# Value products with heads and rests side by side in an attention and MoE kernel

## The chip, the cores and the metric

The kernel runs on one core of a Trainium2 chip. The metric is the device time of one execution in microseconds (us). Engines are named as the profile names them: PE is TensorE's matrix product, PEld its weight load, DVE is VectorE, ACT is ScalarE, POOL is GpSimd and SP is SyncE, which here issues nearly all transfers.

## The reference

Eight batches of eight heads, 512 local and 32 global tokens with 64 elements each. Global queries see all 544 keys, local queries see the 32 global keys and the local keys within 32 positions. All outputs, laid out as 4352 tokens of 512 elements, go through a layer of 2048 with a squared ReLU.

```python
out_g = np.matmul(sm(s_g), v_all)
...
mask = np.abs(pos[:, None] - pos[None, :]) <= window
s_ll = np.where(mask, s_ll, -1000000000.0)
s_l = np.concatenate([s_lg, s_ll], axis=-1)
out_l = np.matmul(sm(s_l), np.concatenate([v_g, v_l], axis=2))
out = np.concatenate([out_g, out_l], axis=2)
...
h = np.maximum(x @ w_in, 0.0)
return (h * h @ w_out).astype(np.float32)
```

## The kernel before

The work is cut into 128 "heads" `t`: a batch, a half of its 512 local queries (256 queries) and one of eight heads. One pass of the main loop is an iteration `t`. In it the kernel computes the scores of head `t`, the transposes and value products of head `t - 1`, and one step `m = t - 9` of the second part, which works on blocks of 256 tokens: eight steps to a block, each with 256 of the 2048 hidden elements (`gemm1`, `act1`, `act2`) and the second layer of the step before (`gemm2`).

Precision comes from splitting. A float32 tensor is written as a head, its value rounded to `fp32r` (a cast on ACT, named `hi`, `ph`, `gh`, `x_h`), and a rest, the difference (a subtraction on DVE, named `lo`, `pl`, `gl`, `x_l`). A product is then head times head, head times rest, and rest times head. The first 16 heads (`plain`) are computed in plain float32 without splits.

For one head from 16 on, the steps are:

- `split_head`: ACT casts the packed queries, keys and values (864 columns) to `hi`; DVE subtracts to make `lo` (448 columns: queries and 192 value columns), the rest of the keys in the lower 64 partitions, and the rest of the global values (32 partitions, 64 columns).
- `scores`: four products into the PSUM tile `s`.
- `softmax1` on DVE (mask, maximum), `softmax2` on ACT (two exponentials with sums), `softmax3` on DVE (reciprocal, two multiplications of 224 columns).
- `transposes` on PE into the one PSUM tile `pt`; `pt_split` on ACT copies the heads to `ph` (four copies), `pt_rest` on DVE makes the rests (`pl`, and parts of `ph`).
- `av`: nine products into the PSUM tile `xa`, six of 128 columns for the two halves, two of 128 and one of 256 columns for the middle keys and the globals.
- `x_evac`: ACT copies `xa` to `x_h`, DVE subtracts to `x_l`; these feed `gemm1`.

The global queries of four heads are handled together, with 16 such groups in all. `g_soft`, `g_exp`, `g_norm`, `g_tr`, `g_tr_last`, `g_rest`, `g_split_v`, `g_av` (13 products of 128 columns) and `g_x` are "jobs", spread over the iterations after the group's last scores by a table of iteration and place. `gt` and `gxo`, the global tiles in PSUM, use the same single buffer (tag `xa`) as the local products.

PE, ACT and DVE run independently, each its own queue in order. From iteration 17 on (`FREE`) each keeps the order in which the program is written; before that a scheduler may reorder. Weights of the second part are decoded and split in the first iterations by a written plan (`PLAN`). `SQ` says in which of 16 iterations the square in `act1` is taken by ACT; in the others DVE multiplies. The order within one iteration, by engine, for heads from 17 on:

```python
# PE:  transposes(t-1), scores(t), gemm1(m,0), gemm1(m,1), av(t-1), g_scores(t), gemm2(m-1)
# ACT: pt_split(t-1), softmax2(t), act1(m), x_evac(t-1), split_head(t+1), g_evac(t), act2(m)
# DVE: softmax1(t), pt_rest(t-1), softmax3(t), act1(m), x_evac(t-1), split_head(t+1), g_evac(t), act2(m)
```

Jobs at place 4 follow `pt_split`, those at 3 follow `pt_rest`, those at 2 stand ahead of `gemm2` and `act2`, those at 1 end the iteration. Every eighth iteration `evac` copies a finished block `o` out on ACT, ahead of `softmax3`.

Of the kernel before, what the change touches and what calls it, by code (L numbers as in the profile page):

```python
# [16 lines left out]
P = 128  # L17
# [14 lines left out]
LOOK = 2  # L32
SQ = (2, 3, 4, 5, 14, 15)
MUL = 9
# [3 lines left out]
def f(ap):  # L38
    return ap.bitcast(F32)
# [19 lines left out]
def attention_moe(  # L59
# [65 lines left out]
    def split_head(t):  # L125

        hd = heads[t]
        raw = hd["raw"]
        if plain(t):
            return  # L130
        hi = p2.tile([P, PK], F32R, tag="hi", name=f"hi{t}")
        lo = p2.tile([P, QC + 192], F32R, tag="lo", name=f"lo{t}")
        ac.copy(hi, raw)
        ve.tensor_sub(lo, raw[:, KC : KC + QC + 192], f(hi[:, KC : KC + QC + 192]))
        ve.tensor_sub(hi[64:, :KC], raw[64:, :KC], f(hi[64:, :KC]))
        ve.tensor_sub(hi[32:64, PK - 64 :], raw[32:64, PK - 64 :], f(hi[32:64, PK - 64 :]))
        hd["hi"], hd["lo"] = hi, lo
# [47 lines left out]
    def softmax3(t):  # L185
        st = heads[t]["st"]
        pr = prob[t % 2]
        ve.tensor_scalar(out=st[:, 6:8], in0=st[:, 4:6], scalar1=1e-9, scalar2=None, op0=ALU.add)
        ve.reciprocal(out=st[:, 0:2], in_=st[:, 6:8])
        for u in range(2):  # L190
            w_ = pr[:, WIN * u : WIN * (u + 1)]
            if MUL <= t < NPLAIN:
                ac.activation(out=w_, in_=w_, func=AF.Copy, scale=st[:, u : u + 1])
            else:
                ve.tensor_scalar(out=w_, in0=w_, scalar1=st[:, u : u + 1], scalar2=None, op0=ALU.mult)
# [6 lines left out]
    def pt_split(t):  # L202
        hd = heads[t]
        if plain(t):
            pts = p2.tile([P, 512], F32, tag="gh", name=f"pts{t}")
            ac.copy(pts, pt)
            hd["pts"] = pts
            return
        ph = p1.tile([P, 640], F32R, tag="ph", name=f"ph{t}")
        pl = p1.tile([P, 256], F32R, tag="pl", name=f"pl{t}")  # L210
        ac.copy(ph[:, :256], pt[:, :256])
        ac.copy(ph[:64, 256:384], pt[:64, 320:448])
        for r in (0, 32):
            ac.copy(ph[r : r + 32, 384:640], pt[64:96, 256:512])
        hd["ph"], hd["pl"] = ph, pl

    def pt_rest(t):
        if plain(t):
            return
        ph, pl = heads[t]["ph"], heads[t]["pl"]  # L220
        ve.tensor_sub(pl, pt[:, :256], f(ph[:, :256]))
        ve.tensor_sub(ph[64:, 256:384], pt[:64, 320:448], f(ph[:64, 256:384]))

        ve.tensor_sub(ph[64:, 384:640], pt[64:, 256:512], f(ph[:64, 384:640]))

    def av(t):
        hd = heads[t]
        c = QC + KC
        if plain(t):

            xa = ps_a.tile([P, HALF], F32, tag="xa", name=f"xa{t}")
            v, pts = hd["raw"][:, c:], hd["pts"]
            mm = [
                (xa, v[:, 0:128], pts[:, 256:512]),
                (xa[:, 0:128], v[:, 64:192], pts[:, 0:128]),
                (xa[:, 128:256], v[:, 128:256], pts[:, 128:256]),
            ]
        else:
            xa = ps_a.tile([64, HALF], F32, tag="xa", name=f"xa{t}")
            vh, vl, ph, pl = hd["hi"][:, c:], hd["lo"][:, QC:], hd["ph"], hd["pl"]  # L240
            mm = []
            for u in range(2):
                o, vs, ps = xa[:, 128 * u : 128 * u + 128], slice(64 * u, 64 * u + 64), slice(128 * u, 128 * u + 128)
                mm += [(o, vh[:, vs], ph[:, ps]), (o, vl[:, vs], ph[:, ps]), (o, vh[:, vs], pl[:, ps])]
            o = xa[:, 64:192]
            mm += [(o, vh[:, 128:192], ph[:, 256:384]), (o, vl[:, 128:192], ph[:, 256:384])]
            mm.append((xa, vh[:, 192:256], ph[:, 384:640]))
        for i, (o, a, b) in enumerate(mm):
            pe.matmul(o, a, b, start=i == 0, stop=i == len(mm) - 1, skip_group_check=True)
        hd["xa"] = xa[:64, :]  # L250

    def x_evac(t):
# [3 lines left out]
        if g == 0:  # L256
            ac.copy(xg[r, h // 2, :], xa)
        else:
            ac.copy(x_h[r, g % 2, h // 2, :], xa)
            ve.tensor_sub(x_l[r, g % 2, h // 2, :], xa, f(x_h[r, g % 2, h // 2, :]))  # L260
        heads[t] = None
# [3 lines left out]
    def g_load(t):  # L265
# [7 lines left out]
        if plain(t):  # L273
            qz = p1.tile([P, 512], F32, tag=("ph", "gvl", "gvh", "ph")[t // 4], name=f"qz{t}")
            nc.gpsimd.memset(qz, 0.0)
# [42 lines left out]
    def g_split_v(t, pair):  # L318

        gv = state["gv"]  # L320
        gvh = p1.tile([P, 5, P], F32R, tag="gvh", name=f"gvh{t}_{pair}")
        gvl = p1.tile([P, 4, P], F32R, tag="gvl", name=f"gvl{t}_{pair}")
        ac.copy(gvh, gv)
        ve.tensor_sub(gvl, gv[:, :4, :], f(gvh[:, :4, :]))
        ve.tensor_sub(gvh[32:64, 4, :], gv[32:64, 4, :], f(gvh[32:64, 4, :]))
        state["gvs"] = gvh, gvl

# [11 lines left out]
    def g_norm(t):  # L339
        s, st = sg[:, (t // 4) % 2, :], state["gst", t]  # L340
        for o in (544, 576):
            ve.tensor_copy(out=s[:, o : o + 32], in_=s[:, 512:544])
        ve.tensor_scalar(out=st[:, 3:4], in0=st[:, 2:3], scalar1=1e-9, scalar2=None, op0=ALU.add)
        ve.reciprocal(out=st[:, 0:1], in_=st[:, 3:4])
        ve.tensor_copy(out=st[:64, 1:2], in_=st[64:, 0:1])

    def g_tr(t):
# [3 lines left out]
        for c in range(4):  # L351
            pe.transpose(gt[:, 128 * c : 128 * c + 128], s[:, 128 * c : 128 * c + 128], ident)
        pth = p1.tile([P, 640], F32R, tag="pth", name=f"pth{t}")
        ac.copy(pth[:, :512], gt)
        state["gpt"] = pth, gt

# [8 lines left out]
    def g_rest(t):  # L365
        (pth, gt), ge = state["gpt"], state["ge"]
        ptl = p1.tile([P, 512], F32R, tag="ptl", name=f"ptl{t}")
        ac.copy(pth[:64, 512:], ge[:64, :])
        ve.tensor_sub(ptl, gt, f(pth[:, :512]))
        ve.tensor_sub(pth[64:, 512:], ge[64:, :], f(pth[:64, 512:]))  # L370
        state["gpt"] = pth, ptl

    def g_av(t, pair):
        (gvh, gvl), (pth, ptl) = state["gvs"], state["gpt"]
        xo = ps_a.tile([64, P], F32, tag="xa", name=f"gxo{t}_{pair}")
        mm = []
        for c in range(4):
            cols = slice(128 * c + 64 * pair, 128 * c + 64 * pair + 64)
            mm += [(pth[:, cols], gvh[:, c, :]), (pth[:, cols], gvl[:, c, :]), (ptl[:, cols], gvh[:, c, :])]
        mm.append((pth[:, 512 + 64 * pair : 576 + 64 * pair], gvh[:, 4, :]))  # L380
        for i, (x, y) in enumerate(mm):
            pe.matmul(xo, x, y, start=i == 0, stop=i == len(mm) - 1)
        xs = p1.tile([64, P], F32, tag="xs", name=f"gxs{t}_{pair}")
        ac.activation(out=xs, in_=xo, func=AF.Copy, scale=state["gst", t][:64, pair : pair + 1])
        state["xs"] = xs
# [56 lines left out]

    def gemm1(m, j):
        blk, st = divmod(m, 8)
# [11 lines left out]
        for n, (a, b) in enumerate(mm):  # L456
            pe.matmul(hp[:, j, :], a, b, start=n == 0, stop=n == len(mm) - 1)

    def act1(m):
# [3 lines left out]
        ac.activation(out=r, in_=hp, func=AF.Relu)  # L463
        if m < 8 or m + LAG < NT + 8 and (m + LAG) % 16 in SQ:
            ac.activation(out=r, in_=r, func=AF.Square)
# [37 lines left out]
    def evac(blk, tiles=(0, 1)):  # L503
        for i in tiles:
            pool, tag = ((p1, "ot"), (p2, "gl"))[i]
            ot = pool.tile([P, DM], F32, tag=tag, name=f"ot{blk}_{i}")
# [82 lines left out]
    for t in range(NSTEP + LAG + 1):  # L589
# [32 lines left out]
        if live and early:  # L622
            g_scores(t)
        if run:
            gemm1(m, 1)
        if prev:
            av(t - 1)
        if live and not early:
            g_scores(t)
        if early and t + 1 < NPLAIN:  # L630
            scores(t + 1)
        if live and not early:
            softmax3(t)
# [137 lines left out]
```

## Time and profile before

| | |
|---|---|
| median of 3 runs | 1068.78 us (1068.65 to 1068.86) |
| profiled execution | 1068.82 us, span 1067.0 us |
| granted TensorE clock | 1.000 |
| busy PE / PEld | 1050.4 / 941.7 us |
| busy DVE / ACT / POOL | 856.3 / 753.1 / 3.9 us |
| moved by DMA | 96.78 MB, mean 91 GB/s |

The span is the time from the first to the last instruction of the program. Busy time is the union of an engine's instructions. Since nearly every instruction is issued through one helper, almost all rows carry line 52 (`L52`), and one reads them by the names of the tiles: `ph<-pt` is an instruction that writes `ph` and reads `pt`. Shapes are partitions times elements. In lists of groups, a row gives the busy time of the group, the mean duration of one instruction in ns, and the idle time of the engine ahead of it with what ended it.

### The profile page before, as it was taken

To read this page: it belongs to the slowest core of one execution; us is meant where nothing else is said; L and a number is where in the kernel's file an instruction comes from. 1 tells how busy PE (TensorE), PEld (TensorE's weight loads), DVE (VectorE), ACT (ScalarE), POOL (GpSimd) and SP (SyncE) were. 2 spreads that over 40 slices of the span, in tenths; PEclk is the share of its full clock that TensorE was granted. 3 is DMA by queue.
4 is the path that set the end of the run, shared out by engine and by line. 5 is a ranking of instruction groups with operands and counts; after the bars stand their busy time and mean duration, and the time that the engine had idled before them with its cause. 6 is when DMAs were issued, how large, how long until landed. Compare 5 with 4: busy or idle time off the path is not lost.

```text
span 1067.0 us, 21142 instructions
## 1 busy us (share of the span) xinstructions
PE 1050.4 (98%) x7568; PEld 941.7 (88%) x7568; DVE 856.3 (80%) x2687; ACT 753.1 (71%) x1901; POOL 3.9 (0%) x14
## 2 busy tenths in 40 slices
PE   7999999999999999999999999999999999999998
PEld 6776889999998989998999989999999989999896
DVE  5698988898888989988888888888888888874321
ACT  5898877778777776778777777777777787774322
POOL 1000000000000000000000000000000000000000
PEclk9999999999999999999999999999999999999999
DMA  9772132223222322222322222223221322201000
GB/s 372 310 263 74 57 106 76 71 80 98 68 89 64 103 65 83 74 91 77 94 71 82 86 72 76 90 66 100 78 89 55 94 86 66 88 29 33 13 20 20
DMA packets 54312, 96.78 MB, mean 91 GB/s; under 512 B 4288, under 2 KB 29376, under 8 KB 54208
## 3 DMA queue, kind: packets, MB, share of 16 engines
q1 hardware_dynamic: 54064, 95.37, 27.2%
q8 instruction: 60, 0.98, 0.4%
q14 instruction: 44, 0.36, 0.1%
q10 hardware_dynamic: 144, 0.07, 0.0%
HBM read 86.51 MB, written 8.91 MB: 89 GB/s over the span
## 4 chain that ended last, share of the span: by engine, by line
PE 87%; ACT 7%; DVE 4%; issue 1%; DMA 0%; ACTq 0%
PE o L52 33%; PE h L52 32%; PE xa L52 7%; PE s L52 6%; PE pt L52 5%; PE gxo L52 2%; PE gs L52 2%; ACT prob L52 1%; DVE prob L52 1%; ACT r L52 1%; ACT ph L52 1%; ACT hi L52 1%; ACT ot L52 1%; PE gt L52 1%; ACT sg L52 0%
## 5 line engine op out<-in xcount | busy, mean ns | idle before, releaser
L52 PE MATMUL h<-x_h,ws 128*128 128x256 f32 x2048 | 388.9, 283 | 0.0
L52 PEld LDWEIGHTS h<-x_h,ws 128*128 128x128 f32 x2048 | 327.0, 191 | 0.5
L52 PE MATMUL o<-ws,gh 128*128 128x512 f32 x1024 | 321.3, 395 | 0.0
L52 PE MATMUL h<-x_l,ws 128*128 128x256 f32 x1024 | 289.1, 282 | 0.1
L52 PEld LDWEIGHTS o<-ws,gh 128*128 128x128 f32 x1024 | 185.5, 188 | 34.6
L52 PE MATMUL o<-ws,gl 128*128 128x512 f32 x512 | 202.6, 396 | 0.0
L52 PEld LDWEIGHTS h<-x_l,ws 128*128 128x128 f32 x1024 | 195.9, 191 | 0.9 <-DVE x_l L52 0.4
L52 ACT CAST ph<-pt 128x256 fp32r<-128x256 f32 x448 | 141.1, 341 | 67.7 <-PE pt L52 60.8
L52 ACT ACTIVATE prob<-prob,st 128x224 f32<-128x224 f32 x270 | 127.8, 475 | 61.2 <-DVE st L52 59.1
L52 ACT ACTIVATE r<-h 128x512 f32<-128x512 f32 x136 | 81.4, 599 | 112.3 <-PE h L52 112.3
L52 PEld LDWEIGHTS o<-ws,gl 128*128 128x128 f32 x512 | 96.2, 188 | 22.7
L52 DVE CUSTOM_DVE_ANT_0 prob<-s,con 128x224 f32<-128x224 f32 x256 | 90.0, 386 | 24.5 <-PE s L52 23.2
L52 DVE TENSOR_TENSOR gl<-r,gh 128x512 fp32r<-128x512 f32 x128 | 87.9, 686 | 23.3 <-ACT gh L52 20.5
L52 ACT CAST hi<-raw 128x864 fp32r<-128x864 f32 x112 | 102.5, 915 | 1.4
L52 DVE TENSOR_TENSOR r<-h,r 128x512 f32<-128x512 f32 x82 | 56.7, 692 | 51.9 <-ACT r L52 50.6
L52 PE MATMUL xa<-ph,hi 128*64 128x128 f32 x448 | 87.3, 238 | 1.6 <-DVE ph L52 1.2
L52 DVE TENSOR_TENSOR hi<-raw,hi 64x352 fp32r<-64x352 f32 x224 | 82.5, 368 | 6.4
L52 ACT CAST gh<-r 128x512 fp32r<-128x512 f32 x128 | 79.1, 618 | 9.1 <-DVE r L52 8.7
L52 DVE TENSOR_TENSOR ph<-pt,ph 64x128 fp32r<-64x128 f32 x224 | 79.6, 355 | 7.0
L52 DVE TENSOR_TENSOR lo<-raw,hi 128x448 fp32r<-128x448 f32 x112 | 69.6, 622 | 15.3 <-ACT hi L52 12.5
L52 PE MATMUL pt<-con,prob 128*128 128x128 f32 (+1 forms) x512 | 78.2, 274 | 0.7 <-ACT prob L52 0.5
L52 DVE TENSOR_SCALAR prob<-prob,st 128x224 f32<-128x224 f32 x242 | 70.7, 334 | 4.1
(80 smaller groups left out, 1572.7 us busy)
## 6 DMA issues: line engine op xcount, KB each, us to landing
raw<-in_pk_dram SPq DMA_DIRECT2D x127, 432.0 KB, 3.2
wr<-in_w_dram SPq DMA_DIRECT2D x32, 512.0 KB, 7.9
gv<-in_vg_dram SPq DMA_DIRECT2D x32, 320.0 KB, 3.3
out_dram<-ot SPq DMA_DIRECT2D x32, 256.0 KB, 2.2
qr<-in_qg_dram SPq DMA_DIRECT2D x31, 64.0 KB, 2.8
out_dram<-ot SPq DMA_DIRECT2D x8, 64.0 KB, 1.7
con<-in_consts_dram SPq DMA_DIRECT2D x2, 224.0 KB, 5.1
raw<-in_pk_dram SPq DMA_DIRECT2D x1, 304.0 KB, 3.2
```

The lines of the kernel that those rows point to most:

```text
L52: r = method(*args, **kwargs)
```

## The change

The value products get their head and rest stored side by side. `pt_split` and `pt_rest` write one tile `ps` of 896 columns in which head and rest of 128 columns alternate, `split_head` writes heads and rests of the values in strips of 64, and one product with a 128-wide weight (head and rest of the values) and a 256-wide moving operand (head and rest of the probabilities) replaces three. `av` then has four products into a 128-partition `xa`, and the partial sums stand in three places, which `x_evac` adds on DVE: one subtraction and two additions in place of one subtraction. `g_av` has five products, and two additions (`g_add`) follow.

Moved: `av` stands between two halves of `gemm1(m, 1)`; `split_head(t + 1)` and `x_evac(t - 1)` stand ahead of `act1`; all squares of iterations up to 127 are taken by ACT, those after it by DVE; the second multiplication of `softmax3` goes to ACT for the split heads; the global scaling becomes `g_mul` on ACT, in place of the scale in the copy of `gxo`; the output staging tile shares a buffer with the global `pth`; one early `qz` uses another buffer.

```diff
-        hi = p2.tile([P, PK], F32R, tag="hi", name=f"hi{t}")
-        lo = p2.tile([P, QC + 192], F32R, tag="lo", name=f"lo{t}")
-        ac.copy(hi, raw)
-        ve.tensor_sub(lo, raw[:, KC : KC + QC + 192], f(hi[:, KC : KC + QC + 192]))
+        c = QC + KC
+        hi = p2.tile([P, c + 2 * VC + QC], F32R, tag="hi", name=f"hi{t}")
+        lo = hi[:, c + 2 * VC :]
+        vr = raw[:, c:].rearrange("p (b n) -> p b n", b=4)
+        vs = hi[:, c : c + 2 * VC].rearrange("p (b n) -> p b n", b=4)
+        ac.copy(hi[:, :c], raw[:, :c])
+        ac.copy(vs[:, :, :64], vr)
+        ve.tensor_sub(lo, raw[:, KC:c], f(hi[:, KC:c]))
         ve.tensor_sub(hi[64:, :KC], raw[64:, :KC], f(hi[64:, :KC]))
-        ve.tensor_sub(hi[32:64, PK - 64 :], raw[32:64, PK - 64 :], f(hi[32:64, PK - 64 :]))
+        ve.tensor_sub(vs[:, :, 64:], vr, f(vs[:, :, :64]))
...
-            if MUL <= t < NPLAIN:
+            if MUL <= t < NPLAIN or t >= NPLAIN and u == 1:
                 ac.activation(out=w_, in_=w_, func=AF.Copy, scale=st[:, u : u + 1])
...
-        ac.copy(ph[:, :256], pt[:, :256])
-        ac.copy(ph[:64, 256:384], pt[:64, 320:448])
-        for r in (0, 32):
-            ac.copy(ph[r : r + 32, 384:640], pt[64:96, 256:512])
+        ps = p1.tile([P, 896], F32R, tag="ph", name=f"ph{t}")
+        pb = ps[:, :512].rearrange("p (u h n) -> p u h n", u=2, h=2)
+        ac.copy(pb[:, :, 0, :], pt[:, :256].rearrange("p (u n) -> p u n", u=2))
+        ac.copy(ps[:64, 512:640], pt[:64, 320:448])
+        ac.copy(ps[:64, 640:], pt[64:, 256:])
...
+        ve.tensor_sub(pb[:, :, 1, :], pt[:, :256].rearrange("p (u n) -> p u n", u=2), f(pb[:, :, 0, :]))
+        ve.tensor_sub(ps[64:, 512:640], pt[:64, 320:448], f(ps[:64, 512:640]))
+        ve.tensor_sub(ps[64:, 640:], pt[64:, 256:], f(ps[:64, 640:]))
...
+            xa = ps_a.tile([P, 512], F32, tag="xa", name=f"xa{t}")
+            xb = xa.rearrange("p (u h n) -> p u h n", u=2, h=2)
+            ps, vs = hd["ps"], [hd["hi"][:, c + 128 * i : c + 128 * i + 128] for i in range(4)]
+            both = bass.AP(xa.tensor, xa.offset + 64, [list(xa.ap[0]), [192, 2], [1, 64]])
+            mm = [(both, vs[2], ps[:, 512:640]), (xb[:, :, 0, :], vs[3], ps[:, 640:])]
+            mm += [(xa[:, 256 * u : 256 * u + 256], vs[u], ps[:, 256 * u : 256 * u + 256]) for u in range(2)]
...
+            ac.copy(x0, xb[:64, :, 0, :])
+            ve.tensor_sub(xr, xb[:64, :, 0, :], f(x0))
+            ve.tensor_add(xr, xb[:64, :, 1, :], xr)
+            ve.tensor_add(x1, xb[64:, :, 0, :], xr)
...
+    def g_mul(t):
+        s, st = sg[:, (t // 4) % 2, :], state["gst", t]
+        ac.activation(out=s[:, :544], in_=s[:, :544], func=AF.Copy, scale=st[:, 0:1])
+        for o in (544, 576):
+            ac.copy(s[:, o : o + 32], s[:, 512:544])
...
         for c in range(4):
-            cols = slice(128 * c + 64 * pair, 128 * c + 64 * pair + 64)
-            mm += [(pth[:, cols], gvh[:, c, :]), (pth[:, cols], gvl[:, c, :]), (ptl[:, cols], gvh[:, c, :])]
-        mm.append((pth[:, 512 + 64 * pair : 576 + 64 * pair], gvh[:, 4, :]))
+            o = 256 * c + 128 * pair
+            mm.append((xo, pts[:, o : o + 128], gvs[:, c : c + 6 : 5, :]))
+        mm.append((xo[:64, 0, :], pts[:, 1024 + 64 * pair : 1088 + 64 * pair], gvs[:, 4, :]))
...
+    def g_add(t, pair):
+        xs, xo = state["xs"]
+        ve.tensor_add(xs, xo[:64, 1, :], xs)
+        ve.tensor_add(xs, xo[64:, 0, :], xs)
...
-        if m < 8 or m + LAG < NT + 8 and (m + LAG) % 16 in SQ:
+        if m + LAG < NT:
             ac.activation(out=r, in_=r, func=AF.Square)
...
-            pool, tag = ((p1, "ot"), (p2, "gl"))[i]
+            pool, tag = ((p1, "pth"), (p2, "gl"))[i]
...
+        late = prev and not plain(t - 1)
         if run:
-            gemm1(m, 1)
+            gemm1(m, 1, 0 if late else None)
         if prev:
             av(t - 1)
+        if run and late:
+            gemm1(m, 1, 1)
...
             softmax3(t)
+        if late:
+            if t + 1 < NT:
+                split_head(t + 1)
+            x_evac(t - 1)
         if run:
             act1(m)
-        if prev:
+        if prev and not late:
             x_evac(t - 1)
...
                 (d + 2, 3, g_norm),
+                (d + 2, 2, g_mul),
...
+                (d + 4, 3, g_add, 0),
                 (max(d + 4, 17), 3, g_x, 0),
...
+                (max(d + 7, 18), 3, g_add, 1),
                 (max(d + 7, 18), 3, g_x, 1),
```

More of the change, by code (lines that the diff above doesn't have):

```diff
@@ L32 @@
 LOOK = 2
-SQ = (2, 3, 4, 5, 14, 15)
 MUL = 9
@@ L208, in pt_split @@
             return
-        ph = p1.tile([P, 640], F32R, tag="ph", name=f"ph{t}")
-        pl = p1.tile([P, 256], F32R, tag="pl", name=f"pl{t}")
-        ac.copy(ph[:, :256], pt[:, :256])
-        ac.copy(ph[:64, 256:384], pt[:64, 320:448])
-        for r in (0, 32):
-            ac.copy(ph[r : r + 32, 384:640], pt[64:96, 256:512])
-        hd["ph"], hd["pl"] = ph, pl
+        ps = p1.tile([P, 896], F32R, tag="ph", name=f"ph{t}")
[3 more added lines that the diff above has]
+        ac.copy(ps[:64, 640:], pt[64:, 256:])
+        hd["ps"], hd["pb"] = ps, pb
     def pt_rest(t):
@@ L219, in pt_rest @@
             return
[L220 to L224, printed above, removed]
+        ps, pb = heads[t]["ps"], heads[t]["pb"]
+        ve.tensor_sub(pb[:, :, 1, :], pt[:, :256].rearrange("p (u n) -> p u n", u=2), f(pb[:, :, 0, :]))
+        ve.tensor_sub(ps[64:, 512:640], pt[:64, 320:448], f(ps[:64, 512:640]))
+        ve.tensor_sub(ps[64:, 640:], pt[64:, 256:], f(ps[:64, 640:]))
     def av(t):
@@ L238, in av @@
         else:
[L239 to L247, printed above, removed]
+            xa = ps_a.tile([P, 512], F32, tag="xa", name=f"xa{t}")
[4 more added lines that the diff above has]
+            mm += [(xa[:, 256 * u : 256 * u + 256], vs[u], ps[:, 256 * u : 256 * u + 256]) for u in range(2)]
         for i, (o, a, b) in enumerate(mm):
             pe.matmul(o, a, b, start=i == 0, stop=i == len(mm) - 1, skip_group_check=True)
-        hd["xa"] = xa[:64, :]
+        hd["xa"] = xa
     def x_evac(t):
@@ L256, in x_evac @@
         if g == 0:
-            ac.copy(xg[r, h // 2, :], xa)
-        else:
-            ac.copy(x_h[r, g % 2, h // 2, :], xa)
-            ve.tensor_sub(x_l[r, g % 2, h // 2, :], xa, f(x_h[r, g % 2, h // 2, :]))
+            ac.copy(xg[r, h // 2, :], xa[:64, :])
+            heads[t] = None
+            return
+        x0, x1 = x_h[r, g % 2, h // 2, :], x_l[r, g % 2, h // 2, :]
+        if plain(t):
+            ac.copy(x0, xa[:64, :])
+            ve.tensor_sub(x1, xa[:64, :], f(x0))
+        else:
+            xb = xa.rearrange("p (u h n) -> p u h n", u=2, h=2)
+            x0, x1 = [x.rearrange("p (u n) -> p u n", u=2) for x in (x0, x1)]
+            xr = p1.tile([P, 2, P], F32, tag="xr", name=f"xr{t}")[r]
+            ac.copy(x0, xb[:64, :, 0, :])
+            ve.tensor_sub(xr, xb[:64, :, 0, :], f(x0))
+            ve.tensor_add(xr, xb[:64, :, 1, :], xr)
+            ve.tensor_add(x1, xb[64:, :, 0, :], xr)
         heads[t] = None
@@ L273, in g_load @@
         if plain(t):
-            qz = p1.tile([P, 512], F32, tag=("ph", "gvl", "gvh", "ph")[t // 4], name=f"qz{t}")
+            qz = p1.tile([P, 512], F32, tag=("ph", "r", "gvh", "ph")[t // 4], name=f"qz{t}")
             nc.gpsimd.memset(qz, 0.0)
@@ L320, in g_split_v @@
         gv = state["gv"]
-        gvh = p1.tile([P, 5, P], F32R, tag="gvh", name=f"gvh{t}_{pair}")
-        gvl = p1.tile([P, 4, P], F32R, tag="gvl", name=f"gvl{t}_{pair}")
+        gvs = p1.tile([P, 9, P], F32R, tag="gvh", name=f"gvh{t}_{pair}")
+        gvh, gvl = gvs[:, :5, :], gvs[:, 5:, :]
         ac.copy(gvh, gv)
@@ L325, in g_split_v @@
         ve.tensor_sub(gvh[32:64, 4, :], gv[32:64, 4, :], f(gvh[32:64, 4, :]))
-        state["gvs"] = gvh, gvl
+        state["gvs"] = gvs
     def g_soft(t):
@@ L339, in g_norm @@
     def g_norm(t):
-        s, st = sg[:, (t // 4) % 2, :], state["gst", t]
-        for o in (544, 576):
-            ve.tensor_copy(out=s[:, o : o + 32], in_=s[:, 512:544])
+        st = state["gst", t]
         ve.tensor_scalar(out=st[:, 3:4], in0=st[:, 2:3], scalar1=1e-9, scalar2=None, op0=ALU.add)
         ve.reciprocal(out=st[:, 0:1], in_=st[:, 3:4])
-        ve.tensor_copy(out=st[:64, 1:2], in_=st[64:, 0:1])
+    def g_mul(t):
[3 more added lines that the diff above has]
+            ac.copy(s[:, o : o + 32], s[:, 512:544])
     def g_tr(t):
@@ L352, in g_tr @@
             pe.transpose(gt[:, 128 * c : 128 * c + 128], s[:, 128 * c : 128 * c + 128], ident)
-        pth = p1.tile([P, 640], F32R, tag="pth", name=f"pth{t}")
-        ac.copy(pth[:, :512], gt)
-        state["gpt"] = pth, gt
+        pts = p1.tile([P, 1152], F32R, tag="pth", name=f"pth{t}")
+        pc = pts[:, :1024].rearrange("p (c h n) -> p c h n", c=8, h=2)
+        gc = gt.rearrange("p (c n) -> p c n", c=8)
+        ac.copy(pc[:, :, 0, :], gc)
+        state["gpt"] = pts, pc, gc
     def g_tr_last(t):
@@ L365, in g_rest @@
     def g_rest(t):
[L366 to L371, printed above, removed]
+        (pts, pc, gc), ge = state["gpt"], state["ge"]
+        ac.copy(pts[:64, 1024:], ge[:64, :])
+        ve.tensor_sub(pc[:, :, 1, :], gc, f(pc[:, :, 0, :]))
+        ve.tensor_sub(pts[64:, 1024:], ge[64:, :], f(pts[:64, 1024:]))
     def g_av(t, pair):
-        (gvh, gvl), (pth, ptl) = state["gvs"], state["gpt"]
-        xo = ps_a.tile([64, P], F32, tag="xa", name=f"gxo{t}_{pair}")
+        gvs, pts = state["gvs"], state["gpt"][0]
+        xo = ps_a.tile([P, 2, P], F32, tag="xa", name=f"gxo{t}_{pair}")
         mm = []
         for c in range(4):
-            cols = slice(128 * c + 64 * pair, 128 * c + 64 * pair + 64)
-            mm += [(pth[:, cols], gvh[:, c, :]), (pth[:, cols], gvl[:, c, :]), (ptl[:, cols], gvh[:, c, :])]
-        mm.append((pth[:, 512 + 64 * pair : 576 + 64 * pair], gvh[:, 4, :]))
-        for i, (x, y) in enumerate(mm):
-            pe.matmul(xo, x, y, start=i == 0, stop=i == len(mm) - 1)
-        xs = p1.tile([64, P], F32, tag="xs", name=f"gxs{t}_{pair}")
-        ac.activation(out=xs, in_=xo, func=AF.Copy, scale=state["gst", t][:64, pair : pair + 1])
+            o = 256 * c + 128 * pair
+            mm.append((xo, pts[:, o : o + 128], gvs[:, c : c + 6 : 5, :]))
+        mm.append((xo[:64, 0, :], pts[:, 1024 + 64 * pair : 1088 + 64 * pair], gvs[:, 4, :]))
+        for i, (o, x, y) in enumerate(mm):
+            pe.matmul(o, x, y, start=i == 0, stop=i == len(mm) - 1, skip_group_check=True)
+        xs = p1.tile([64, P], F32, tag="xs", name=f"gxs{t}_{pair}")
+        ac.copy(xs, xo[:64, 0, :])
+        state["xs"] = xs, xo
+    def g_add(t, pair):
+        xs, xo = state["xs"]
+        ve.tensor_add(xs, xo[:64, 1, :], xs)
+        ve.tensor_add(xs, xo[64:, 0, :], xs)
         state["xs"] = xs
@@ L441, in attention_moe, with gemm1 @@
     moe = {}
-    def gemm1(m, j):
+    def gemm1(m, j, half=None):
         blk, st = divmod(m, 8)
@@ L456, in gemm1 @@
         for n, (a, b) in enumerate(mm):
-            pe.matmul(hp[:, j, :], a, b, start=n == 0, stop=n == len(mm) - 1)
+            if half in (None, 2 * n // len(mm)):
+                pe.matmul(hp[:, j, :], a, b, start=n == 0, stop=n == len(mm) - 1)
     def act1(m):
@@ L633, in attention_moe @@
             softmax3(t)
+        if late:
+            if t + 1 < NT:
+                split_head(t + 1)
+            x_evac(t - 1)
         if run:
             act1(m)
-        if prev:
+        if prev and not late:
             x_evac(t - 1)
-            if plain(t - 1):
-                w_take(-1)
+            w_take(-1)
         if early:
@@ L642, in attention_moe @@
         w_tick(t, 1)
-        if t + 1 < NT:
+        if t + 1 < NT and not late:
             split_head(t + 1)
@@ L729 @@
             pk[:, hf, :, 64 * dup : 64 * dup + 64, c + 128 : c + 192] = vw[:, :, 128:192]
-        for dup in range(3):
-            pk[:, hf, :, 32 * dup : 32 * dup + 32, c + 192 : c + 256] = v_g
+        for dup in range(2):
+            pk[:, hf, :, 64 * dup : 64 * dup + 32, c + 192 : c + 256] = v_g
     pk = pk.reshape(NT, P, PK)
```

## The prediction

> **What bounds the kernel now.** I read the engine shares and the chain first, then one whole period of the steady part, then who waits inside it. The page:
>
> ```profile
> PE 1050.4 (98%) x7568; PEld 941.7 (88%) x7568; DVE 856.3 (80%) x2687; ACT 753.1 (71%) x1901; POOL 3.9 (0%) x14
> PE 87%; ACT 7%; DVE 4%; issue 1%; DMA 0%; ACTq 0%
> ```
>
> TensorE looks like the only limit. The share is a mean over unlike stages, though, so I cut out one period. Iterations 81 to 96 (16 heads) begin with their four `pt` transposes at 598.64 us, and iteration 97 begins at 720.92. The windows give that period and all iterations that the change touches (17 to 128), and the waits inside the period follow, DVE's and then PE's:
>
> ```profile
> 598.64:720.92 122.28, 121.91 (x928) 111.52 (x926) 106.74 (x341) 90.79 (x234) 0.00 (x0) 1.00 0.26 81
> 106.97:958.12 851.15, 847.39 (x6425) 773.25 (x6424) 744.21 (x2368) 632.83 (x1631) 0.00 (x0) 1.00 0.25 79
> ```
>
> ```profile
> DVE lo L52 <- ACT hi L52: 1.9, 6, 0.4
> DVE x_l L52 <- ACT x_h L52: 1.8, 3, 0.7
> DVE prob L52 <- PE s L52: 1.5, 3, 0.8
> DVE r L52 <- ACT r L52: 1.5, 4, 0.5
> DVE gvl L52 <- ACT gvh L52: 1.3, 2, 0.6
> DVE pth L52 <- ACT pth L52: 1.0, 2, 0.8
> ```
>
> ```profile
> PE s L52 <- ACT sg L52: 0.2, 1, 0.2
> PE xa L52 <- DVE ph L52: 0.2, 1, 0.2
> ```
>
> The columns after the time of a window are busy PE, PEld, DVE, ACT. PE is busy 121.91 of 122.28 at granted clock 1.00 and waits 0.4. But DVE waits only 9.0 (the six lines added); the remaining 113.3 it works or stands in the short gaps between its instructions, since 106.74 is busy. So two engines are nearly full, and DVE has 9.0 us of air per 16 heads, 0.56 a step. From iteration 17 on every engine keeps its written order, so a new wait on DVE can't be filled by later work. The change takes from PE and rearranges DVE; the question is DVE's queue.
>
> **PE's part.** A regular step's value products and what stands around them:
>
> ```profile
> 541.89 0.28 PE L52 MATMUL h<-x_h,ws 128*128 128x256 f32 x1
> 542.00 0.22 PE L52 MATMUL xa<-ph,hi 128*64 128x128 f32 x1
> ...
> 542.48 0.28 PE L52 MATMUL xa<-ph,hi 128*64 128x256 f32 x1
> 542.60 0.30 PE L52 MATMUL gs<-hi,qgz 128*128 128x288 f32 x1
> ```
>
> Eight starts of 128 columns lie 0.06 apart (542.00 to 542.48), one of 256 takes 0.12 (to 542.60): 9 local products take 8 x 0.06 + 0.12 = 0.60. After, one of 128 and three of 256: 0.06 + 0.36 = 0.42, so 0.18 saved a head, 2.9 a period. The 128-wide weights cost nothing: the `h` products load such weights and start 0.11 to 0.12 apart, as the last one here does before `xa`. A global product goes from 13 x 0.06 = 0.78 to 4 x 0.12 + 0.06 = 0.54; four in a period save 1.0. PE alone would need 122.3 - 3.9 = 118.4. Two local products write two separate runs of columns, which no matmul of this trace does; bounds are no extra cost and that of doubling those two (0.18 a head, 2.9 a period). I take none, and even doubling leaves PE at 121.3, below what DVE needs below.
>
> The PSUM page of the Trainium skill ("PSUM — Partial Sum Buffer", Specifications) says that a non-contiguous access pattern slows matmuls significantly; by that rule PE keeps 121.3 instead of 118.4. No run here shows it yet.
>
> **DVE's part.** Rows of the period by shape (busy, mean ns, idle before), and below them six of ACT from the whole run:
>
> ```profile
> L52 DVE TENSOR_TENSOR lo<-raw,hi 128x448 fp32r<-128x448 f32 x16 | 10.0, 622 | 2.3 <-ACT hi L52 1.9
> L52 DVE TENSOR_SCALAR prob<-prob,st 128x224 f32<-128x224 f32 x32 | 9.3, 334 | 0.6
> L52 DVE TENSOR_TENSOR r<-h,r 128x512 f32<-128x512 f32 x10 | 6.9, 692 | 1.7 <-ACT r L52 1.5
> L52 DVE TENSOR_TENSOR pl<-pt,ph 128x256 fp32r<-128x256 f32 x16 | 6.7, 421 | 0.1
> L52 DVE TENSOR_TENSOR x_l<-xa,x_h 64x256 fp32r<-64x256 f32 x16 | 6.6, 414 | 2.1 <-ACT x_h L52 1.8
> L52 DVE TENSOR_TENSOR hi<-raw,hi 32x64 fp32r<-32x64 f32 x17 | 3.6, 215 | 0.5
> L52 DVE TENSOR_TENSOR pth<-gs,pth 64x128 fp32r<-64x128 f32 x2 | 0.6, 294 | 1.0 <-ACT pth L52 1.0
> L52 DVE COPY sg<-sg 128x32 f32<-128x32 f32 x4 | 0.5, 179 | 0.1
> L52 DVE COPY gst<-gst 64x1 f32<-64x1 f32 x2 | 0.3, 150 | 0.1
> ```
>
> ```profile
> L52 ACT ACTIVATE prob<-prob,st 128x224 f32<-128x224 f32 x270 | 127.8, 475 | 61.2 <-DVE st L52 59.1
> L52 ACT CAST hi<-raw 128x864 fp32r<-128x864 f32 x112 | 102.5, 915 | 1.4
> L52 ACT CAST gvh<-gv 128x640 fp32r<-128x640 f32 x32 | 23.0, 718 | 0.0
> L52 ACT ACTIVATE sg<-sg,gst 128x544 f32<-128x544 f32 x16 | 11.9, 746 | 0.0
> L52 ACT CAST ph<-pt 32x256 fp32r<-32x256 f32 x224 | 82.0, 366 | 4.1
> L52 ACT COPY ot<-o 128x512 f32<-128x512 f32 x34 | 18.5, 589 | 3.6 <-PE o L52 3.0
> ```
>
> Work per period of 16 steps. All squares of these iterations go to ACT: 10 x 0.692 = -6.9. One of the two scalings of `prob` goes to ACT; the pair takes 0.58 (row below), one alone 0.334: 16 x 0.25 = -4.0. `x_evac` reads the bank three times instead of once: 32 x 0.414 = +13.2. `split_head`: the `lo` subtraction shrinks to 256 columns (0.42 by the `pl` row) and the 32x64 one becomes 128x256 (0.215 to 0.42): -0.20 + 0.21 = 0. `pt_rest` and `g_rest` keep sizes, written in strips: 0. Globals: four 32-column copies and two 64x1 go (-1.0), eight 64x128 additions come (+2.4): +1.4. Sum +3.7, so 113.3 becomes 117.0.
>
> Now the waits, in a regular step (iteration 73):
>
> ```profile
> 540.72 0.74 DVE L52 TENSOR_TENSOR ph<-pt,ph 64x128 fp32r<-64x128 f32 x2
> 541.49 0.17 DVE L52 TENSOR_SCALAR st<-st 128x2 f32<-128x2 f32 x1
> 541.70 0.17 DVE L52 RECIPROCAL st<-st 128x2 f32<-128x2 f32 x1
> 541.90 0.58 DVE L52 TENSOR_SCALAR prob<-prob,st 128x224 f32<-128x224 f32 x2
> 542.89 0.69 DVE L52 TENSOR_TENSOR r<-h,r 128x512 f32<-128x512 f32 x1 [0.41 <-ACT r L52]
> ```
>
> After the scaling DVE's next work is today `r` and `x_l`, and ACT makes `hi` meanwhile. In the new order the next work on DVE is `lo`, which needs ACT's `hi`, and on ACT `hi` stands behind the scaling that moved there, which needs DVE's reciprocal. Laid out: the reciprocal ends at 541.87, ACT scales 541.91 to 542.39 (0.475), the cast of 608 columns takes about 0.69 (915 at 864 and 718 at 640 columns give 0.88 ns a column) and starts about 0.09 before the scaling ends, as ACT's neighbours overlap: ends 542.99, `lo` starts 543.03. DVE's own scaling is done at 542.24. That is 0.79 of idle DVE in every step: 16 x 0.79 = 12.6. Nothing can stand there, whatever comes ahead of the reciprocal moves both. Ends: nothing (if it fell together with a wait that is counted) and 0.79; I take 0.79, each piece has its row.
>
> Other waits of a period: `gvl` on `gvh` stays, 1.3; `pth` on ACT falls from 1.0 to about 0.4, as `pt_split` has three copies for four; the wait for the scores stays, 1.5; those of `r`, `x_l` go. Twice a period ACT evacuates `o` (two copies, 0.59 each) before it scales, which delays `lo` by about 0.55: 1.1. Twice `g_mul` (0.75 and two small copies) stands ahead of `gh`, so `gl` comes about 0.6 late: 1.2.
>
> Sum: 117.0 + 12.6 + 1.3 + 0.4 + 1.5 + 1.1 + 1.2 = 135.1 per 16 heads, against 122.28 now and PE's 118.4. So DVE sets the pace and PE waits, first at the value products, which also stand six `h` matmuls (0.72) earlier: in this step `ph` is ready at 541.46, while their new place is 541.89 - 5 x 0.12 = 541.29. Behind them wait the other six `h`, `gs` and the second layer.
>
> ACT, busy 90.79, gains ten squares (7 at DVE's price), 16 scalings (7.6), a second cast for `hi` (about 0.2 a head by the same line through 640 and 864) and `g_mul`, and loses a 0.37 copy a head (-5.9): some 105, under 135. Costed at nothing: the output staging moves to the buffer of `pth`, whose last reader (`g_av`, iterations 1 and 7 of 16) is a step and more before the copies (2 and 10), and whose next writer (3 and 13) comes a step later while the transfer lands in 2.2 us; no DMA of SP is moved past another, POOL gets nothing, the first 16 heads keep their code, and after iteration 128 (from 958) DVE is busy 31.49 of 109.00, so the squares there cost nothing.
>
> ```profile
> 958.00:1067.00 109.00, 103.69 (x683) 92.95 (x681) 31.49 (x64) 33.68 (x61) 0.00 (x0) 1.00 0.07 21
> ```
>
> ```profile
> out_dram<-ot SPq DMA_DIRECT2D x32, 256.0 KB, 2.2
> ```
>
> **The number.** +12.8 per 122.28 us, over 851.15 us: 6.96 periods, +89. The profiled execution took 1068.82 (span 1067.0 and 1.8 around it), within 0.04 of the median: 1158.
>
> **Rivals.** First, faster: PE stays the bound. PE's share of 98% and its 87% of the chain speak for it. The "Perfetto Trace Analysis" page of the Trainium skill (Identifying the Most-Contended Engine) says to relieve the engine of highest occupancy first, which by the busy shares is PE; whether that holds here is what DVE's 9.0 us decide. Then 3.9 x 6.96 = 27 are won: 1042, or 1055 to 1062 if the earlier products wait 0.14 to 0.2 a step for `ph`. It needs DVE's waits to sum to under 122.3 - 117.0 = 5.3 a period, for instance if ACT's cast were ready when the reciprocal ends; the written order of ACT speaks against it.
>
> Second, slower still: the bank `xa`. The global transposes and products (six places a period) need it free, now after three DVE reads at the end of a longer DVE queue. Today this costs almost nothing:
>
> ```profile
> PEld gxo L52 <- DVE x_l L52: 0.4, 2, 0.2
> ```
>
> If DVE's later work in turn waits for these (`g_rest`, the additions), 6 x 0.8 = 5 come on top: 140, and 1068.8 + 17.7 x 6.96 = 1192.
>
> Third, no change: half of the 0.79 is overlap that I don't see and the other waits go: 117.0 + 6.3 - 1 = 122.3.
>
> **How the numbers follow.** DVE-bound as summed 0.74 (1115 to 1195 by the ends of the smaller waits), still slower 0.09, faster 0.14, no change 0.03. A change under 0.2% (2 us) can't be told from none. Slower is 0.83. The range 1075 to 1195 leaves out the faster case and a part of the worst.
>
> **What would show it.** Right: DVE's `lo` waits for ACT `hi` in nearly all of 112 heads, 0.7 to 0.9 each; a mean step of about 8.4 us against 122.28 / 16 = 7.64; PE's waits at `xa` and `gxo` for DVE, in sum over 80; xa starts 0.12 apart where not waiting. Wrong: `lo` waits under 0.3, or a DVE whose period stays under 122; `xa` matmuls more than 0.12 apart would show the cost of the two runs of columns.

## The result and the profile after

The changed kernel takes 1186.62 us (median of 4, 1186.37 to 1188.63) against 1068.72 us: a ratio of 1.1107 with an interval of 1.109 to 1.1123. It is 118 us slower, within the range of the prediction and above its 1158. The page of the changed kernel, shares of the engines and of the chain:

```profile
PE 1071.5 (90%) x6752; PEld 931.4 (79%) x6752; DVE 896.7 (76%) x2750; ACT 825.2 (70%) x2126; POOL 3.9 (0%) x14
DVE 43%; PE 27%; ACT 21%; issue 8%; DMA 1%; ACTq 0%; DVEq 0%
```

No engine is full any more, and the chain that was 87% PE now passes between DVE, PE and ACT. The windows give the same 16 heads as before the change (iterations 81 to 96), all iterations that the change touches, and the stretch after them. After the time come busy PE, PEld, DVE and ACT:

```profile
667.82:806.49 138.67, 124.51 (x816) 109.53 (x815) 111.89 (x349) 101.38 (x267) 0.00 (x0) 1.00 0.23 71
106.69:1075.91 969.22, 869.03 (x5647) 763.83 (x5646) 779.23 (x2422) 705.94 (x1851) 0.00 (x0) 0.99 0.23 69
1075.91:1184.60 108.69, 102.84 (x653) 92.24 (x651) 36.95 (x74) 31.52 (x60) 0.00 (x0) 0.99 0.07 21
```

A period grew from 122.28 to 138.67, and the touched iterations from 851.15 to 969.22: the whole 118. The last stretch is as long as before. The growth is uneven: counted from the first `pt` transpose of one iteration to that of the next, two of the 16 steps (iterations 84 and 94) grow from 8.63 to 11.16, while the eight steps that took 7.3 take 7.4 to 8.5. In the period DVE waits for

```profile
DVE hi L51 <- ACT hi L51: 13.7, 16, 1.3
DVE prob L51 <- PE s L51: 3.4, 4, 1.1
DVE gvh L51 <- ACT gvh L51: 1.3, 2, 0.6
DVE gl L51 <- ACT gh L51: 1.1, 2, 0.6
DVE pth L51 <- ACT pth L51: 0.8, 2, 0.4
```

20.3 us in all, where it was 9.0. (`lo` is now a part of the tile `hi`, so the first line is the wait of `lo`.) Every one of the 16 heads has the wait for `hi`; in the whole run it is 94.7 us, 110 times. One regular step, the reciprocal to `lo` on DVE and the same time on ACT:

```profile
743.19 0.17 DVE L51 RECIPROCAL st<-st 128x2 f32<-128x2 f32 x1
743.39 0.34 DVE L51 TENSOR_SCALAR prob<-prob,st 128x224 f32<-128x224 f32 x1
744.55 0.43 DVE L51 TENSOR_TENSOR hi<-raw,hi 128x256 fp32r<-128x256 f32 x1 [0.82 <-ACT hi L51]
```

```profile
743.45 0.48 ACT L51 ACTIVATE prob<-prob,st 128x224 f32<-128x224 f32 x1 [0.50 <-DVE st L51]
743.83 0.99 ACT L51 CAST hi<-raw 128x608 fp32r<-128x608 f32 x2
```

ACT waits for the reciprocal, scales, casts, and DVE stands idle from 743.73 to 744.55. PE's own waits, over the whole run:

```profile
PE xa L51 <- DVE ph L51: 46.4, 137, 1.8
PE gxo L51 <- DVE x_l L51: 26.8, 15, 2.7
PE xa L51 <- DVE gxs L51: 15.8, 25, 0.6
PE gt L51 <- DVE sg L51: 5.9, 7, 1.6
```

The second line belongs to the two long steps. In iteration 84 the global product waits for DVE's third reading of the local result, since both use the one buffer `xa`; `pt` and `s` stand behind it on PE, and DVE then waits for the scores:

```profile
705.50 0.77 PE L51 MATMUL gxo<-gvh,pth 128*128 128x256 f32 x5 [1.78 <-DVE x_l L51]
707.19 0.39 DVE L51 CUSTOM_DVE_ANT_0 prob<-s,con 128x224 f32<-128x224 f32 x1 [1.12 <-PE s L51]
```

### The profile page after: what moved, and what is told of

Its sections match the earlier page's. It is cut to its first block, busy times and chain, and to the rows that moved or that the text cites. A ratio compares the mean times of both kernels' runs of the same rounds, so it can differ in the third digit from the quotient of the medians.

```text
span 1184.6 us, 19788 instructions
## 1 busy us (share of the span) xinstructions
PE 1071.5 (90%) x6752; PEld 931.4 (79%) x6752; DVE 896.7 (76%) x2750; ACT 825.2 (70%) x2126; POOL 3.9 (0%) x14
## 4 chain that ended last, share of the span: by engine, by line
DVE 43%; PE 27%; ACT 21%; issue 8%; DMA 1%; ACTq 0%; DVEq 0%
PE o L51 10%; DVE hi L51 8%; PE h L51 8%; DVE prob L51 6%; ACT hi L51 6%; DVE ph L51 6%; DVE xr L51 5%; ACT prob L51 4%; DVE st L51 4%; DVE gl L51 4%; PE xa L51 3%; ACT r L51 2%; PE s L51 2%; PE gxo L51 2%; ACT sg L51 2%
## 5 line engine op out<-in xcount | busy, mean ns | idle before, releaser
L51 PE MATMUL h<-x_h,ws 128*128 128x256 f32 x2048 | 408.4, 284 | 0.0
L51 ACT ACTIVATE prob<-prob,st 128x224 f32<-128x224 f32 x382 | 181.8, 478 | 218.3 <-DVE st L51 218.2
L51 DVE TENSOR_TENSOR hi<-raw,hi 128x256 fp32r<-128x256 f32 x336 | 153.8, 458 | 99.7 <-ACT hi L51 94.7
L51 PE MATMUL xa<-ph,hi 128*128 128x128 f32 x448 | 93.8, 301 | 62.7 <-DVE ph L51 46.4
L51 PEld LDWEIGHTS xa<-ph,hi 128*128 128x128 f32 x448 | 65.4, 188 | 88.7 <-issue 39.0
L51 DVE TENSOR_TENSOR ph<-pt,ph 128x256 fp32r<-128x256 f32 x336 | 126.5, 376 | 5.2 <-ACT ph L51 0.7
L51 ACT CAST ph<-pt 128x256 fp32r<-128x256 f32 x336 | 100.3, 333 | 17.9 <-PE pt L51 13.9
L51 ACT CAST hi<-raw 128x608 fp32r<-128x608 f32 x224 | 111.2, 544 | 0.0
L51 DVE TENSOR_TENSOR gl<-r,gh 128x512 fp32r<-128x512 f32 x128 | 88.1, 688 | 20.3 <-ACT gh L51 18.4
L51 PE MATMUL s<-hi 128*128 128x224 f32 x448 | 78.2, 297 | 0.1
L51 ACT ACTIVATE r<-r 128x512 f32<-128x512 f32 x119 | 75.1, 631 | 3.7
```

Source lines behind the costliest of these rows:

```text
L51: r = method(*args, **kwargs)
```

## Experiments

The theory on record was that DVE's queue sets the pace and that its wait for `hi` is the largest new piece. The rivals: PE's new place of the products, or the bank `xa`. Times are medians; "period" is that of the same 16 heads. Except where said, each run is the changed kernel (1186.62, period 138.67) with one edit.

**Scaling back on DVE.**

```diff
-            if MUL <= t < NPLAIN or t >= NPLAIN and u == 1:
+            if MUL <= t < NPLAIN:
```

> The changed kernel with the second scaling of the softmax back on DVE, all else as changed. Theory (DVE's queue sets the pace, and its wait for ACT's cast of the next head, 13.7 us of a 138.7 us period, comes from the scaling on ACT ahead of that cast): DVE works 16 x 0.25 = 4.0 more a period, the wait falls to about 1.4 (the two steps in which ACT evacuates an output block first), so 138.7 - 12.3 + 4.0 = 130.4 a period, over 6.96 periods -58: about 1129. Rival (the early value products or the bank xa set the pace, the wait for the cast is only where DVE's air shows): no gain, 1187, or up to 1214 if the scaling is added to DVE's queue and no wait goes.

Measured 1140.81, period 132.78. In the period:

```profile
DVE hi L51 <- ACT hi L51: 4.2, 9, 0.7
DVE prob L51 <- PE s L51: 3.4, 4, 1.1
```

The wait fell from 13.7 to 4.2, not to 1.4, and the period by 5.9 where 8.3 was expected. The theory's direction holds, and the wait does cost time.

**Local products late again.**

```diff
-            gemm1(m, 1, 0 if late else None)
+            gemm1(m, 1)
         if prev:
             av(t - 1)
-        if run and late:
-            gemm1(m, 1, 1)
```

> The changed kernel with the local value products after all of the first layer's products of the step, as before the change, all else as changed. Theory (DVE's queue sets the pace; PE only waits at the products because it is ahead): the waits move elsewhere, 1187 within 6. Rival (PE's place of the products costs): PE's and PEld's waits at xa for DVE's rests, over 100 us in the whole trace, go for the larger part: 1100 to 1140.

Measured 1192.70. PE's waits at `xa` are a symptom: with the products in their old place the time is not shorter but 6 longer. In the whole run the waits at `xa` for `ph` fall from 46.4 to 30.1, and those at `gxo` for `x_l` rise from 26.8 to 47.8.

**No additions.** The two `tensor_add` of `x_evac` are left out, and the subtraction writes `x_l`.

> The changed kernel without the two additions on DVE when a local result is taken from its bank, so the partial sums of the rests are missing in the result; all else as changed. Theory (DVE's queue sets the pace): 32 x 0.45 = 14.4 us a period go, 138.7 - 14.4 = 124.3, over 6.96 periods -100: about 1087, a little more where PE's 118.4 and its waits begin to bind. Rival (PE's order or products set the pace): within 10 of 1187.

Measured 1148.26, period 133.50: the period fell by 5.2, not 14.4. This is the run against which the first theory fails. DVE is busy 98.64 where it was 111.89, and waits more:

```profile
DVE hi L51 <- ACT hi L51: 13.7, 16, 1.3
DVE gl L51 <- ACT gh L51: 6.8, 8, 1.1
DVE gvh L51 <- ACT gvh L51: 3.5, 5, 0.7
DVE sg L51 <- ACT sg L51: 3.4, 8, 0.4
```

These and two smaller lines sum to 30.3, where it was 20.3. What DVE no longer works it waits for, mostly for ACT, whose cast `gh` ends the step. And ACT waits for DVE in the same period, about twice a step: for the mask and for the reciprocal.

```profile
ACT prob L51 <- DVE st L51: 26.7, 29, 2.0
```

So it isn't one full queue. These waits read as a chain that passes to and fro within a step: mask (DVE), exponentials (ACT), reciprocal (DVE), scaling, cast, square, `gh` (ACT), `gl` (DVE), next mask. That is the second theory; the runs that follow try its links.

**Result taken from its bank ahead of the next split.**

```diff
         if late:
+            x_evac(t - 1)
             if t + 1 < NT:
                 split_head(t + 1)
-            x_evac(t - 1)
```

> The changed kernel with the taking of the local result from its bank ahead of the next head's split on ACT and DVE. Theory (DVE's queue): the wait of 0.83 ahead of the rests of the split goes, as the cast now runs under the subtraction and the additions; in its place DVE waits about 0.55 for ACT's scaling and copy of the result: -0.28 a step, 4.5 a period, -31: about 1155. Rival (the bank xa, held until the third read, sets the pace): it comes free 1.4 us earlier, and PE's waits at the global products and transposes (12.2 us a period) go: about 1100.

Measured 1146.56, period 133.44. The wait changed its name and shrank from 13.7 to 10.5, and a 1100 by the bank alone did not come:

```profile
DVE xr L51 <- ACT x_h L51: 10.5, 16, 1.1
DVE gl L51 <- ACT gh L51: 1.8, 2, 0.9
DVE prob L51 <- PE s L51: 1.1, 2, 0.7
```

The bank has a part all the same. Read earlier, it comes free earlier: PE's wait at `gxo` for `x_l` falls from 26.8 to 0.7 in the whole run, and DVE's wait for the scores from 3.4 to 1.1 a period. That is 2.3 of the 5.2 that the period fell.

**Global additions right behind their product**, at place 1 of the same iteration in place of place 3 of the next.

```diff
-                (d + 4, 3, g_add, 0),
+                (d + 3, 1, g_add, 0),
...
-                (max(d + 7, 18), 3, g_add, 1),
+                (max(d + 6, 17), 1, g_add, 1),
```

> The changed kernel with the two additions of each global result right behind the product, at the end of its iteration, in place of the next iteration behind the local rests. The first theory (DVE's queue alone) fell with the run without additions: DVE lost 14.4 us of work a period and the period only 5.2. Second theory: a step is one chain that passes between DVE and ACT (mask, exponentials, reciprocal, scaling, cast of the next head, square, head of the square, its rest), and beside it global work holds single steps back, here the bank xa: four steps of 16 last 8.0 us because the local products, placed early, wait until the additions have read the global result. Then these fall to about 7.3: 4 x 0.7 = 2.8 a period, -20: about 1166. If the bank is only a wait that another replaces: 1187; if DVE now stands waiting for the product at the end of the step: up to 1200.

Measured 1168.35, period 136.46. The line "PE xa <- DVE gxs" of the changed kernel (15.8, 25 times) is gone: there a global result that stays in the bank until the next iteration's place 3 holds up the early local products. DVE's waits of the period lose their line for the scores (3.4), and one for the copy `gxs` (1.2) comes in its place:

```profile
DVE hi L51 <- ACT hi L51: 13.7, 16, 1.3
DVE gvh L51 <- ACT gvh L51: 1.3, 2, 0.6
DVE gxs L51 <- ACT gxs L51: 1.2, 3, 0.5
DVE gl L51 <- ACT gh L51: 1.1, 2, 0.6
DVE pth L51 <- ACT pth L51: 0.8, 2, 0.4
```

These sum to 18.1, and the 2.2 less is the whole gain of the period. It does not come from scores that are ready earlier, since the global product ahead of them waits as before (26.8 there):

```profile
PE gxo L51 <- DVE x_l L51: 26.6, 15, 2.4
```

DVE now makes the additions in the time in which it stood waiting for those scores.

**Scaling on DVE and no additions** (the first and third edit together).

> The changed kernel with the second scaling back on DVE and without the two additions of the local result, so the partial sums of the rests are missing in the result. First theory (DVE's queue alone): 132.8 - 14.4 = 118.4 a period, PE's own need: 1045 to 1050. Second theory (chain through DVE and ACT, and the global steps): the chain loses the scaling's wait and the additions, but the global steps stay long, about 126 a period: about 1095.

Measured 1108.51, period 128.41: far from the 1045 to 1050 of a single full queue, and 13 above the second theory's estimate.

**One half of the change each.** The local half with the global jobs of before, and the global half in the kernel before (functions and job table swapped whole).

> The local half of the change alone (value products of heads, split, scaling, squares, order within the step), the global products and their jobs as before. First theory: DVE's work falls by the additions of the globals, and the wait at the square's rest goes: -2.5 a period, about 1169. Second theory: the places of the global work in the changed kernel cost some 8 a period (bank held for the additions, transposes that wait for the scaling on ACT), and the thirteen products cost PE 1.0 again: about 1135.

> The global half of the change alone in the kernel before: five products, scaling on ACT ahead of the transposes, additions a slot later; heads as before. DVE gets 1.4 us of work a period and has 9.0 of air, PE is relieved of 1.0. If these places of the global work cost only where the local products stand early and DVE is full: 1062 to 1072. If they cost by themselves (the transposes wait for the scaling, the bank for the additions): 4 to 8 a period, 1090 to 1125.

Measured 1174.61 (period 137.30) and 1076.74 (period 123.91). The local half costs 106, the global half 8. Both runs fell beside what was expected. In the local half the first theory's terms came as it had them: DVE is busy 110.42 where it was 111.89, and the wait of `gl` is gone. But DVE waits longer for the scores, although no global addition is left in the kernel:

```profile
DVE prob L51 <- PE s L51: 4.3, 4, 1.3
```

The places of the global work cost little by themselves, and taking them out of the full change saves 12, not 50.

**Three places undone together** (the edits of the first, fourth and fifth run).

> The changed kernel with three places undone together: second scaling on DVE, local result taken from its bank ahead of the next split, global additions right behind their product. Alone they gave -5.9, -5.2 and -2.2 us a period. The first two both act on DVE's wait for the cast (13.7): together they can give at most that wait less the 4.0 of work, -9.7, and the bank -2.2: 138.7 - 11.9 = 126.8, about 1104. If the chain through ACT and DVE binds in another place still, less: 1115 to 1130. If DVE's queue alone binds: its work of 122.4 and the small waits, about 126, 1098.

Measured 1104.53, period 127.43, as expected. DVE now waits 5.9 in a period:

```profile
DVE gl L51 <- ACT gh L51: 1.5, 2, 0.8
DVE xr L51 <- ACT x_h L51: 1.4, 7, 0.5
DVE gvh L51 <- ACT gvh L51: 1.3, 2, 0.6
DVE pth L51 <- ACT pth L51: 0.8, 2, 0.4
DVE prob L51 <- PE s L51: 0.6, 2, 0.4
DVE gxs L51 <- ACT gxs L51: 0.3, 1, 0.3
```

With these it is near full: 121.5 of 127.4 is work and short gaps. By that share the first theory's picture fits here, and the next run asks what the work is worth.

**The three undone, and no additions.**

> The changed kernel with the three places undone (scaling on DVE, result taken from its bank ahead of the split, global additions at once) and without the two additions of the local result, so the partial sums of the rests are missing in the result. With the places undone DVE waits 6.1 of 127.4 us a period and works or steps between instructions for 121.3. If that work is what is left of the loss, taking 14.4 of it leaves 107, and PE's own need of 118.4 sets the pace with a few us of waits: 119.5 to 121.5 a period, -41 to -55 against 1104.5: 1050 to 1064, below the kernel before, by PE's saving. If the chain between DVE and ACT still binds, as in the run without additions alone (5.2 of 14.4): 1068 to 1075.

Measured 1078.45 (ratio to before 1.0093, 1.0076 to 1.011), period 123.81: not below the kernel before. The additions were worth 26 us here, but PE's saving did not appear. PE is nearly full again while DVE waits 16.2 a period, and the eight steps that took 7.3 before the change take 7.3 again. The period, a regular step's value products in this run, and those of a step in the run with the products late, one that does not wait:

```profile
604.01:727.82 123.81, 121.33 (x816) 109.52 (x814) 102.53 (x333) 94.10 (x251) 0.00 (x0) 1.00 0.25 80
```

```profile
691.75 0.28 PE L51 MATMUL h<-x_h,ws 128*128 128x256 f32 x1
691.87 0.78 PE L51 MATMUL xa<-ph,hi 128*128 128x128 f32 x4
692.49 0.28 PE L51 MATMUL h<-x_h,ws 128*128 128x256 f32 x1
```

```profile
659.49 0.63 PE L51 MATMUL xa<-ph,hi 128*128 128x128 f32 x4
659.96 0.29 PE L51 MATMUL gs<-hi,qgz 128*128 128x288 f32 x1
```

Start to next start is 0.47 without a wait (659.49 to 659.96), where 0.42 was summed, and 0.62 in the early place (691.87 to 692.49), where the rests are not yet ready: DVE's last one ends at 691.91, and the second product needs it.

```profile
691.48 0.43 DVE L51 TENSOR_TENSOR ph<-pt,ph 64x256 fp32r<-64x256 f32 x1
```

The nine products took 0.60. So in the early place the four products save nothing, even with DVE relieved. No run has them late with DVE relieved, where their 0.47 could count.

**A version from these runs.** Value heads and rests side by side, but the probabilities' heads and rests as two products into the same columns: six products, one addition. Scalings on DVE, squares on ACT, bank first, globals as before; `av` early in the first and late in the second.

```diff
+            mm = [(xa[:, 128 * u : 128 * u + 128], vs[u], ps[:, 256 * u : 256 * u + 128]) for u in range(2)]
+            mm += [(xa[:64, 128 * u : 128 * u + 128], vs[u][:, :64], ps[:, 256 * u + 128 : 256 * u + 256]) for u in range(2)]
+            mm += [(xa[:, 64:192], vs[2], ps[:, 512:640]), (xa, vs[3], ps[:, 640:])]
```

> A version made from what the runs show. Local products: value heads and rests stand side by side as weights, but the probabilities' heads and rests are two products into the same columns (six products, PE's time the same 0.42), so the partial sums stand in two places and DVE has one addition, not two. Both scalings on DVE, all squares of these iterations on ACT, the result taken from its bank ahead of the next split, global products as before the change. DVE's work 113.3 - 6.9 + 7.1 = 113.5 a period, PE 119.4 of 122.3 now. With DVE's waits no larger than before (9.0): 122.5, 1070; with half of them: 119.4 to 120, 1050 to 1056. I expect 1062.

> The same version with the local products after all of the first layer's products of the step. If the early place only brings waits of PE, a little faster than the version beside it; if it frees the result sooner for DVE, 3 to 8 us slower. I expect 1066.

Measured 1073.67 (1.0047, 1.003 to 1.0064) and 1072.81 (1.004, 1.0025 to 1.0054): the best of the variants, and no gain on before. Both are slower than the 1062 and 1066 expected, and the 0.9 between them is too little to prefer a place. PE is the bound again, 121.98 busy of 122.74 in the second, and the six products take 0.57, not 0.42. That is 2.4 more a period than the 119.4 of the expectation, so 121.8:

```profile
600.25:722.99 122.74, 121.98 (x879) 111.16 (x878) 107.16 (x346) 92.22 (x245) 0.00 (x0) 1.00 0.26 80
```

```profile
666.64 0.74 PE L51 MATMUL xa<-ph,hi 128*128 128x128 f32 x6
667.21 0.29 PE L51 MATMUL gs<-hi,qgz 128*128 128x288 f32 x1
```

## Why the prediction was right, and which steps were off

Point by point, per period of 16 heads:

| step | predicted | measured |
|---|---|---|
| DVE working or in short gaps | 117.0 | 138.67 - 20.3 = 118.4 |
| wait of `lo` for `hi`, with the delay by `evac` | 12.6 + 1.1 | 13.7 |
| wait for the scores | 1.5 | 3.4 |
| `gvl` (now `gvh`) on ACT | 1.3 | 1.3 |
| `gl` for `gh`, by `g_mul` | 1.2 | 1.1 |
| `pth` on ACT | 0.4 | 0.8 |
| period | 135.1 | 138.67 |
| all iterations, change | +89 | +118 |

The layout of one step gave an idle 0.79; it is 0.82. The sum came out 3.6 short a period: 1.4 of work, 1.9 of waiting for the scores and 0.4 at `pth`, less 0.1 at `gl`. The wait for the scores was taken over unchanged. It is the term that was mis-sized most, and it comes from the bank `xa`: the scores stand behind a global product that waits for the third reading of the local result. Reading the bank earlier takes the wait from 3.4 to 1.1; without any global addition it is still 4.3. So the second rival, the bank, was a part of the truth, and the measured 1186.62 lies nearer to its 1192 than to 1158. The touched time grew by 118 and not by 6.96 x 16.4 = 114, because the first 16 of these iterations, in some of which weights are still being decoded and split, grew by 19.9 (from 124.62 to 144.54).

The reason was less exact than the sum. The work and the waits of one engine add up to the period whichever engine sets the pace; so the terms that agree show that DVE's waits were laid out rightly, and not that DVE alone holds the kernel. "DVE sets the pace" is not what the runs show: with 14.4 of its work gone the period fell by 5.2. The waits are handed to and fro between DVE and ACT, and an idle stretch on one is mostly the other's work on the same chain. Nor was "nothing can stand there" true: in another order the taking of the bank stands there in part, and the run is 40 us shorter.

On PE, 118.4 a period was too low. Four products take 0.47 and not 0.42, so 0.13 are saved a head and not 0.18, and "the 128-wide weights cost nothing" holds only behind 256 moving columns, as the last section shows. In the early place, the 0.14 to 0.2 that stood in the faster rival is paid (0.15), and nothing is left. With 0.47 PE alone needs 122.3 - 2.1 - 1.0 = 119.2 a period, so the faster rival's 1042 becomes about 1047, an estimate, even with a DVE that never holds PE up; the run with three places undone and no additions ended at 1078.45.

Where the time went, by the runs in order: the three places undone together take the period from 138.67 to 127.43 (-11.2), the additions from there to 123.81 (-3.6), and 1.5 remain to 122.28. Undone alone, the scaling gave 5.9, the order of split and bank 5.2, the addition slot 2.2. What holds the last 1.5 was not tried separately; 1.0 of it lies in the two steps in which `g_rest` and the global split stand ahead of the softmax, 9.14 where they took 8.63. The place of `split_head` ahead of `act1` and the squares on ACT were not undone either, but the last versions keep both at periods of 122.8 and 122.7.

The signs that the prediction named: `lo` waits in all 16 heads of the period, as said; PE's waits for DVE at `xa` and `gxo` sum to 46.4 + 26.8 + 15.8 = 89, over 80; the mean step is 138.67 / 16 = 8.67, against 8.4. Where nothing waits (the step at 659.49 above), the four products start 0.06, 0.17 and 0.12 apart, and the first two write separate runs of columns. The 0.17 is not the cost of those runs: in the version of six products the same product writes one run, and the next starts 0.17 behind it too (667.04 to 667.21). The last section says what it is. The PSUM page of the Trainium skill ("PSUM — Partial Sum Buffer", Specifications) would have those products slower; for runs of 64 and 128 columns this trace does not show it, and the measurement decides. The 121.3 that the prediction put beside that rule is its own bound of doubling.

## What to carry to other kernels

Beside the busy share of the fullest engine, count in one steady period how much the next engine waits: here DVE's 9.0 us of 122, with nothing that could fill a new wait under a written order. Moving work from one in-order engine to another is not free when both hand a result back within the same step; lay out that one step on both engines, from the rows, before counting the work moved. And products placed earlier are only worth something when their operands are early too.

## What the hardware showed that was not expected

A product with a 128-column weight is not always as cheap as its moving columns. Behind 256 moving columns such weights are hidden (the `h` products, 0.12 apart). Behind 128 they are not: the six products of the last version, five of them with 128 moving columns, take 0.57 where 0.42 was summed from 0.06 and 0.12. The starts of the weight loads in that run, medians over 112 heads, show where the 0.15 goes. While a product of 128 moving columns runs, a load of 128 columns holds the next load off until 0.11 after its own start, and one of 64 columns until 0.06 after it. Three of the six loads are such wide ones, each 0.05 longer than the moving columns beside it. Of the four products one has such a load, and they take 0.47 for 0.42. The nine products of the kernel before had weights of 64 columns and stayed at 0.06.

The page "TensorE: Matmul & The Clock Gate" of the Trainium skill (LDWEIGHTS) gives a weight load by its columns; by its rule 128 columns take 107 ns, an estimate. The trace agrees with its 0.11 between the starts of two loads.
